# Memory at the borders between two kinds of layer, reused tile by tile

## The chip, the cores and the metric

The kernel runs on one core of one Trainium2 chip. The core has a matrix engine (TensorE: PE for the matmuls, PEld for its weight loads), a vector engine (DVE), a scalar engine (ACT), a general engine (POOL) and a sync engine (SP) whose work here is to issue DMAs. Each engine works through its own instructions in order. A DMA is issued by an engine (ACTq, SPq in the profile) and then runs by itself. The metric is the device time of one execution in microseconds (us); lower is better.

## The reference

Four layers over 2048 tokens of 640 numbers, in the order A, B, A, B; each layer is `x = x + layer(layernorm(x))`. Both kinds walk through the tokens in segments and carry a memory along.

```python
# A: 32 heads of 20, 4 segments of 512 tokens
for s in range(4):
    p = softmax(q_s k_s^T * scale + causal_mask);  a_dot = p @ v_s
    a_mem = (phi(q_s) @ M) / (phi(q_s) @ z + 1e-6)
    o_s = g * a_mem + (1 - g) * a_dot
    M += phi(k_s)^T @ v_s;  z += sum(phi(k_s))
return concat(o) @ wo
# B: 32 heads of 128, 64 segments of 32 tokens, memory of 8 rows
mem = mem0
for s in range(64):
    h = concat([mem, x_s])                      # 40 rows
    q, k, v = h @ Wq, h @ Wk, h @ Wv            # each 640 x 4096
    p = softmax(q k^T * scale masked);  o = (p @ v) @ Wo
    mem = o[:8];  out_s = o[8:]
```

A step of B needs the memory rows that the step before has made, so its 64 steps are a chain. A's last segment has no memory to hand on.

## The kernel before

**Layer A** (`layer_A`) takes a segment of 512 tokens as four tiles of 128. `seg_load` loads a tile (`a_xt`) and normalizes it (`a_xn`), `seg_tr` transposes it (`a_tps`) into `a_xnT`. Eight groups of four heads follow; a group projects Q, K, V (`a_QP`, `a_KP`, `a_VP`), spreads Q over a masked tile by four small DMAs (`a_qTm`), and works through four heads: scores `a_S`, softmax `a_Pj`, transposes `a_tpA`/`a_tpB`, `a_PVu`. The memory (`a_MZ`, `a_MZb`) is brought up to date in the first three segments only. A finished segment goes through an out stage per tile: `out_stage_a` loads the residual (`a_xr`) and transposes the result (`a_otps`, copied by ACT to `a_oT`), `out_stage_b` multiplies by Wo (`a_YP`), adds the residual (`a_xnew`) and stores it twice, as float32 (`xres`) and as bfloat16 (`xres_bf`), which is what B reads. The last segment's four out stages are A's drain. A scheduler sets the order of A's instructions on every engine.

**Layer B** (`layer_B`) has a prologue and 64 steps. The order of its instructions on PE, ACT, DVE and POOL is written out by hand, and all of them carry line 100 in the profile; the scheduler places only its DMAs on SP. B's Wq and Wk stay resident: they are loaded during the first layer. Wv and Wo (5.24 MB each) are loaded anew for each B. The prologue:

1. loads four tiles of x (`b_xt`), issues the loads of Wv and Wo on ACT's queue (`load_B_weights`), normalizes two tiles, transposes them (`b_lntps`); ACT copies them to `b_HX` (24 rows per step) and `b_TX` (the last 8 rows of each of 8 steps, the tails); five small DMAs bring in `mem0`.
2. The tails of the first 8 steps are projected with Wq and Wk in eight units (`b_tail`), evicted by ACT and DVE in turn to `b_tu` and stored to memory outside the core (`b_QKd`), from where each step takes its rows (`b_tl`).
3. K and Q of step 0 (`b_Kp`, `b_Qp`), evicted to `b_kq`, transposed (`b_TP`) and scattered to `b_KT` and `b_QT`.
4. The tails' V in eight units (`b_vtail`), evicted to `b_vt`, each stored by two DMAs (`b_VTd`); then V of step 0 (`b_V`), and the first unit of the next 8 steps.

Step 0 proper begins with the matmuls `b_Ka`, `b_Qa`, `b_Kb`, `b_Qb`. A step ends with the projection by Wo (`b_OPS`); the tail rows' own projection is deferred (`b_OPSd`), added to what was stored (`b_XOd`, a load, an add, a store).

A tile framework hands out memory. A pool holds tiles, and a tile name with `bufs` buffers makes the tile wait for the last use of the one `bufs` back. When a layer ends its pools are released, and a new pool on the same memory waits for the whole released pools below it. Both `b_tu` and `b_vt` have one buffer. At the border from B to A, A's four weights are loaded on ACT's queue (`load_A_weights`).

Of the kernel before, what the change touches and what calls it, by code (L numbers as in the profile page):

```python
# [28 lines left out]
D = 640  # L29
NCH = 5  # L30
# [105 lines left out]
def alloc_A_weights(tc, ctx, W):  # L136
    wp = ctx.enter_context(tc.tile_pool(name="a_w", bufs=1))
    W.wq = wp.tile([128, NCH, 32, 32], BF16, name="a_wq_pad")
    W.wk = wp.tile([128, NCH, 32, 32], BF16, name="a_wk_pad")
    W.wv = wp.tile([128, NCH, D], BF16, name="a_wv")  # L140
    W.wo = wp.tile([128, NCH, D], BF16, name="a_wo")


def load_A_weights(nc, W, A_wq, A_wk, A_wv, A_wo, padded, stage):

    first = not padded
    eng = nc.sync if first else nc.scalar
    for nm, src, pad in (("wq", A_wq, W.wq), ("wk", A_wk, W.wk)):
        if first:
            raw = stage[nm]  # L150
            nc.gpsimd.memset(pad[:, :, :, 20:32], 0.0)
            nc.vector.tensor_copy(pad[:, :, :, 0:20], raw.rearrange("p c (h d) -> p c h d", d=20))
        else:
            nc.scalar.dma_start(pad[:].rearrange("p c h s -> p (c h s)"), padded[nm])
    eng.dma_start(W.wv[:], A_wv.rearrange("(c p) n -> p c n", p=128))
    eng.dma_start(W.wo[:], A_wo.rearrange("(c p) n -> p c n", p=128))
# [8 lines left out]
def layer_A(nc, tc, C, W, x_src, x_dst, src_is_bf16, nseg=4, out_bf16=False, xb_dst=None, load_w=None, side_loads=None):  # L165
# [7 lines left out]
    with ExitStack() as ctx:  # L173
        st = ctx.enter_context(tc.tile_pool(name="a_state", bufs=1))
        seg = ctx.enter_context(tc.tile_pool(name="a_seg", bufs=2))
        wk = ctx.enter_context(tc.tile_pool(name="a_wk", bufs=2))
        w1 = ctx.enter_context(tc.tile_pool(name="a_wk1", bufs=1))
        up = ctx.enter_context(tc.tile_pool(name="a_unit", bufs=3))
        up2 = ctx.enter_context(tc.tile_pool(name="a_unit2", bufs=3))
        sm = ctx.enter_context(tc.tile_pool(name="a_sm", bufs=4))  # L180
        pg = ctx.enter_context(tc.tile_pool(name="a_pg", bufs=2, space=PSUM))
        pss = ctx.enter_context(tc.tile_pool(name="a_pss", bufs=3, space=PSUM))
        ppt = ctx.enter_context(tc.tile_pool(name="a_ppt", bufs=3, space=PSUM))

        MZ32 = st.tile([128, 8, 128], F32, name="a_MZ32")
        nc.vector.memset(MZ32[:], 0.0)
        MZb = st.tile([128, 8, 128], BF16, name="a_MZb")
        vaug = [st.tile([128, 4, 4, 32], BF16, name=f"a_vaug{i}") for i in range(2)]
        phik = [st.tile([128, 4, 4, 32], BF16, name=f"a_phik{i}") for i in range(2)]
# [6 lines left out]
        qTm_t = [st.tile([128, 4, 512], BF16, name=f"a_qTm{i}") for i in range(2)]  # L196
# [9 lines left out]
        def seg_load(n_, tt):  # L206
            d = SEG.setdefault(n_, {"xn": [None] * 4, "oT": [None] * 4, "xr": [None] * 4})
            r0 = n_ * 512 + tt * 128
            xt = wk.tile([128, D], BF16 if src_is_bf16 else F32, name="a_xt")
            nc.sync.dma_start(xt[:], x_src[r0:r0 + 128, :])  # L210
            xn = wk.tile([128, D], BF16, name="a_xn")
            layernorm_tile(nc, sm, C, xt[:], xn[:], "a_ln")
            d["xn"][tt] = xn

        def seg_tr(n_, tt):
            d = SEG[n_]
            if "xnT" not in d:
                d["xnT"] = seg.tile([128, NCH, 512], BF16, name="a_xnT", tag="xnT")
# [12 lines left out]
        def out_stage_a(n_, tt):  # L231
            d = SEG[n_]
            r0 = n_ * 512 + tt * 128
            xr = wk.tile([128, D], BF16 if src_is_bf16 else F32, name="a_xr")
            nc.sync.dma_start(xr[:], x_src[r0:r0 + 128, :])
            oT = wk.tile([128, NCH, 128], BF16, name="a_oT")
# [6 lines left out]
        def out_stage_b(n_, tt):  # L243
# [3 lines left out]
            if src_is_bf16:  # L247
                xnew = w1.tile([128, D], F32, name="a_xnew")
            else:
                xnew = xr  # L250
# [8 lines left out]
            xnb = w1.tile([128, D], BF16, name="a_xnb")  # L259
# [5 lines left out]
        for n in range(nseg):  # L265
            xnT = SEG[n]["xnT"]
            Onat = seg.tile([128, 4, D], BF16, name="a_Onat", tag="Onat")
# [45 lines left out]
            def proj_b(G):  # L313
# [9 lines left out]
                if n <= nseg - 2:  # L323
# [4 lines left out]
                    EK = w1.tile([128, 4, 4, 20], F32, name="a_EK")  # L328
# [66 lines left out]
            def PV_evac(u):  # L395
# [7 lines left out]
                if j == 3 and n <= nseg - 2:  # L403
                    upm = w1.tile([128, 128], F32, name="a_upm")
# [125 lines left out]
def layer_B(nc, tc, C, W, x_src, xb_src, x_dst, mem0, B_Wv, B_Wo, nsteps=64, out_bf16=False, tag=""):  # L530
# [7 lines left out]
    with ExitStack() as ctx:  # L538
        st = ctx.enter_context(tc.tile_pool(name="b_state", bufs=1))
        hp = ctx.enter_context(tc.tile_pool(name="b_hx", bufs=4))  # L540
        w2 = ctx.enter_context(tc.tile_pool(name="b_w2", bufs=2))
        wk = ctx.enter_context(tc.tile_pool(name="b_wk", bufs=1))
        sm = ctx.enter_context(tc.tile_pool(name="b_sm", bufs=2))
        kqp = ctx.enter_context(tc.tile_pool(name="b_kqp", bufs=4))
        pp = ctx.enter_context(tc.tile_pool(name="b_ps", bufs=5, space=PSUM))
        po = ctx.enter_context(tc.tile_pool(name="b_po", bufs=1, space=PSUM))
# [4 lines left out]
        selm = st.tile([128, 2, 8], BF16, name="b_sel")  # L551
        nc.vector.tensor_tensor(out=selm[:, 0, :], in0=C.identb[:, 24:32], in1=C.identb[:, 88:96], op=ALU.add)
        nc.vector.tensor_tensor(out=selm[:, 1, :], in0=C.identb[:, 56:64], in1=C.identb[:, 120:128], op=ALU.add)
        OTdef = [st.tile([128, 32, 32], BF16, name=f"b_OTdef{i}") for i in range(2)]
        XO = st.tile([64, 320], F32, name="b_XO")
        nc.vector.memset(XO[:], 0.0)
        XOd = st.tile([64, 320], F32, name="b_XOd")
        mask8 = st.tile([128, 8, 40], BF16, name="b_mask8")

        Px = st.tile([128, 16, 32], BF16, name="b_Px")  # L560
        Pm = st.tile([128, 16, 32], BF16, name="b_Pm")
        nc.gpsimd.memset(Px[:], 0.0)
        nc.gpsimd.memset(Pm[:], 0.0)
        negs = wk.tile([128, 32], F32, name="b_negs", tag="PTa")
        nc.vector.memset(negs[:], -1e9)
        maskf = wk.tile([128, 40], F32, name="b_maskf", tag="OTsb")
        nc.vector.memset(maskf[:], 0.0)

        for hh in range(2):
            m = maskf[64 * hh:64 * hh + 32, :]  # L570
            nc.gpsimd.affine_select(out=m[:, 0:32], in_=negs[64 * hh:64 * hh + 32, :],
                                    pattern=[[1, 32]], compare_op=ALU.is_gt, fill=0.0, base=0, channel_multiplier=-1)
            nc.gpsimd.affine_select(out=m[:, 8:32], in_=m[:, 8:32],
                                    pattern=[[0, 24]], compare_op=ALU.is_gt, fill=0.0, base=-7, channel_multiplier=1)
            nc.gpsimd.affine_select(out=m[:, 0:8], in_=m[:, 0:8],
                                    pattern=[[0, 8]], compare_op=ALU.is_gt, fill=-1e9, base=8, channel_multiplier=-1)
        nc.vector.tensor_copy(mask8[:], maskf[:].unsqueeze(1).to_broadcast([128, 8, 40]))
        HXz = st.tile([128, NCH, 1, 32], BF16, name="b_HXz")
        nc.gpsimd.memset(HXz[:], 0.0)
# [22 lines left out]
        def ln_norm(g):  # L602
            xt = ln_xt[g]
            layernorm_tile(nc, sm, C, xt[:], xt[:], "b_ln")
            ln_ready.append(g)

        def ln_spread(g):
# [6 lines left out]
            if half == 0:  # L614
                TX[T] = w2.tile([128, NCH, 8, 8], BF16, name="b_TX", tag="TX")
# [35 lines left out]
        def tails_load(s):  # L651
            tl = wk.tile([128, 2, 32, 8], BF16, name="b_tl", tag="tl")
# [73 lines left out]
        homes = [(wk, "xt"), (wk, "OTsb"), (w2, "KT"), (w2, "QT")]  # L726
# [3 lines left out]
        load_B_weights(nc, W, B_Wv, B_Wo)  # L730
# [27 lines left out]
        tails_copy(0, tails_load(0))  # L758
        for k in range(8):
            vtail_evac(0, k, vtail_unit(0, k), "dve" if k % 2 == 0 else "act")  # L760
# [329 lines left out]
```

## Time and profile before

| what | time |
|---|---|
| three runs | 3260.51, 3264.31, 3271.95 us (median 3264.31) |
| profiled execution | 3267.92 us, of which the span (first to last instruction) is 3266.2 us |
| PE busy, share of the span | 2860.3 us, 88% |
| DVE, ACT, POOL busy | 59%, 53%, 19% |
| DMA moved | 164.33 MB, 50 GB/s on average |

The span in 40 slices, each digit the busy share in tenths, and the clock that TensorE was granted:

```profile
PE   6888984999999999998869888849999999999987
PEclk9999996999999999999979999969999999999998
```

The slices dip at three places beside the start. These are the borders between layers: A to B near 470 to 575 us, B to A near 1625 to 1675, and A to B again near 2100 to 2210. A layer of A takes some 430 to 450 us, one of B some 1050.

### The profile page before, as it was taken

Reading aid. Unit: us, or ns where it says so; the run is one execution under the profiler, and the core shown is the slowest. Engines: PE = TensorE matmul, PEld = TensorE weight load, DVE = VectorE, ACT = ScalarE, POOL = GpSimd, SP = SyncE. Lnnn points to the kernel's source line nnn. Section 1 sums busy time; section 2 is a strip of 40 time slices with the busy share of each in tenths; the row PEclk is TensorE's granted clock in tenths of the full one; section 3 lists DMA queues with packets and bytes.
Section 4 is the critical chain, followed back from the end, with each engine's and each line's share of the span. In section 5 each row is a group of like instructions: output and inputs, shape, how many; then the busy total and the mean of one; then the engine's idle time right before and its main releaser. Section 6 shows DMA issues by size and latency. Waiting matters only on the chain.

```text
span 3266.2 us, 137871 instructions
## 1 busy us (share of the span) xinstructions
PE 2860.3 (88%) x59517; PEld 1849.8 (57%) x59612; DVE 1921.2 (59%) x5213; ACT 1720.6 (53%) x3840; POOL 615.9 (19%) x1398
## 2 busy tenths in 40 slices
PE   6888984999999999998869888849999999999987
PEld 4666653555555555555446666535555555555544
DVE  6899871555455555544468998715554555555544
ACT  4888871444444444443349888714444444444432
POOL 2133320111111111111111333201111111111111
PEclk9999996999999999999979999969999999999998
DMA  5111115111121111111030111251111111111100
GB/s 189 59 38 42 37 56 166 38 40 40 39 43 39 39 41 41 36 33 27 20 105 20 58 47 43 69 162 33 41 37 37 40 37 37 39 39 35 35 22 17
DMA packets 334865, 164.33 MB, mean 50 GB/s; under 512 B 249520, under 2 KB 322992, under 8 KB 331184
## 3 DMA queue, kind: packets, MB, share of 16 engines
q1 hardware_dynamic: 321680, 119.80, 15.5%
q10 hardware_dynamic: 12576, 35.72, 3.0%
q8 instruction: 467, 7.65, 1.0%
q14 instruction: 142, 1.16, 0.1%
HBM read 95.65 MB, written 51.38 MB: 45 GB/s over the span
## 4 chain that ended last, share of the span: by engine, by line
PE 45%; ACT 14%; DVE 11%; issue 6%; POOL 4%; DMA 4%; SPq 1%; POOLq 0%; DVEq 0%; ACTq 0%
PE b_OPS L100 9%; PE b_Ka L100 5%; PE b_Qb L100 4%; PE b_Qa L100 4%; PE b_Kb L100 4%; ACT a_Pj L351 4%; PE b_OTP L100 3%; DVE b_SP L100 3%; ACT b_KT L100 2%; ACT b_QT L100 2%; PE b_OPSd L100 2%; POOL b_Px L100 2%; ACT b_kq L100 2%; PE b_vtail L100 2%; POOL b_Pm L100 2%
## 5 line engine op out<-in xcount | busy, mean ns | idle before, releaser
L100 PEld LDWEIGHTS <-b_HX 128*32 128x32 bf16 x15360 | 390.2, 97 | 426.2 <-DVE b_HX L100 44.0
L351 ACT ACTIVATE a_Pj<-a_S,a_negm 128x128 bf16<-128x128 f32 (+3 forms) x1024 | 510.4, 549 | 58.3 <-DVE a_negm L350 52.7
L350 DVE TENSOR_REDUCE a_negm<-a_S 128x1 f32<-128x128 f32 (+3 forms) x1024 | 467.0, 482 | 75.7 <-PE a_S L348 42.1
L100 POOL TENSOR_TENSOR b_Px<-b_E,b_rs 128x256 bf16<-128x256 bf16 x128 | 78.7, 615 | 1427.4 <-DVE b_rs L100 1415.4
L346 PE MATMUL a_S<-a_kT,a_qTm 128*128 128x128 bf16 (+3 forms) x1024 | 293.5, 298 | 54.0 <-ACT a_Pj L351 40.0
L100 PE MATMUL b_OPS<-b_wo,b_OTsb 128*32 128x320 bf16 x8192 | 318.0, 309 | 13.4 <-DVE b_OTsb L100 6.4
L100 PEld LDWEIGHTS <-b_OTsb 128*32 128x32 bf16 x8192 | 215.4, 100 | 113.4 <-DVE b_OTsb L100 45.7
L100 DVE CAST b_HX<-b_MT 128x40 bf16<-128x40 f32 x124 | 24.8, 200 | 391.1 <-PE b_MT L100 391.1
L361 PE MATMUL a_tpA<-c_identb,a_Pj 128*128 128x128 bf16 x2048 | 241.1, 218 | 12.9 <-ACT a_Pj L351 3.9
L348 PE MATMUL a_S<-c_negu,c_identb 128*128 128x128 bf16 x1024 | 220.5, 218 | 0.0
L100 ACT CAST b_msb<-b_OPS 128x320 bf16<-128x320 f32 x126 | 53.6, 425 | 303.5 <-PE b_OPS L100 303.5
L100 ACT CAST b_OTsb<-b_OTP 128x320 bf16<-128x320 f32 x256 | 96.5, 429 | 185.9 <-PE b_OTP L100 185.9
L100 ACT CAST b_kq<-b_Kb 128x512 bf16<-128x512 f32 x128 | 74.9, 585 | 202.3 <-PE b_Kb L100 202.3
L100 PE MATMUL b_Ka<-b_wk,b_HX 128*32 128x512 bf16 x2520 | 162.2, 387 | 21.7 <-DVE b_HX L100 21.6
L361 PEld LDWEIGHTS <-a_Pj 128*128 128x128 bf16 x2048 | 149.1, 97 | 56.5 <-issue 14.3
L348 PEld LDWEIGHTS <-c_identb 128*128 128x128 bf16 x1024 | 98.8, 97 | 129.2 <-issue 101.1
L100 DVE TENSOR_SCALAR b_kq<-b_Qa 128x512 bf16<-128x512 f32 x128 | 88.5, 692 | 139.4 <-PE b_Qa L100 138.7
L100 ACT ACTIVATE b_E<-b_SP 128x320 bf16<-128x320 f32 x256 | 111.9, 437 | 95.9 <-DVE b_SP L100 89.0
L100 PE MATMUL b_Qa<-b_wq,b_HX 128*32 128x512 bf16 x2520 | 159.4, 382 | 0.0
L100 PE MATMUL b_Va<-b_wv,b_HX 128*32 128x512 bf16 x2520 | 159.1, 381 | 0.0
L100 DVE CAST b_OTsb<-b_OTP 128x320 bf16<-128x320 f32 x256 | 113.7, 486 | 76.4 <-PE b_OTP L100 76.4
L100 PEld LDWEIGHTS <-b_kq 128*128 128x128 bf16 x2080 | 117.7, 98 | 71.7 <-ACT b_kq L100 55.2
(195 smaller groups left out, 6307.5 us busy)
## 6 DMA issues: line engine op xcount, KB each, us to landing
b_QKd<-b_tu SPq DMA_DIRECT2D x128, 128.0 KB
b_tl<-b_QKd SPq DMA_DIRECT2D x128, 128.0 KB
b_wv<-in_B_Wv_dram ACTq DMA_DIRECT2D x2, 5120.0 KB
b_wo<-in_B_Wo_dram ACTq DMA_DIRECT2D x2, 5120.0 KB
a_qTm<-a_qT SPq DMA_DIRECT2D x256, 32.0 KB
b_VTd<-b_vt SPq DMA_DIRECT2D x256, 32.0 KB
b_Vth<-b_VTd SPq DMA_DIRECT2D x512, 16.0 KB
b_XO<-xres SPq DMA_DIRECT2D x256, 30.0 KB
```

Of the source, the lines that this page charges most:

```text
L100: r = f(*a, **k)
L346: nc.tensor.matmul(Sx[:, 0:N], lhsT=stt["qTm"][:, j, 128 * qc:128 * qc + 128], rhs=kT[:, 0:N], start=True, stop=False)
L348: nc.tensor.matmul(Sx[:, N - 128:N], lhsT=C.identb[:], rhs=C.negu[:], start=False, stop=True)
L350: nc.vector.tensor_reduce(out=negm[:], in_=Sx[:, 0:N], axis=AX.X, op=ALU.max, negate=True)
L351: nc.scalar.activation(out=Pj[:, OFFS[qc]:OFFS[qc] + N], in_=Sx[:, 0:N], func=ACT.Exp, bias=negm[:, 0:1], scale=1.0)
L361: nc.tensor.transpose(tpA[:, bi, :], Pj[:, OFFS[qc] + 128 * kc: OFFS[qc] + 128 * kc + 128], C.identb[:])
```

## The change

- All pools of both layers are made with `reuse_waits="tile"`: a new tile waits for the tiles that lay on its addresses, no longer for whole pools. The pools stand in a new order, and tiles are put into other pools, so that the addresses of one layer's early tiles are those of the other layer's early-freed tiles. The separate functions that laid out the weights are gone; `layer_A` and `layer_B` do it.
- B's Wv is loaded in five pieces of 1 MB, Wo in eight of 640 KB, A's weights as before in four; all on SP's queue and none on ACT's.
- The first four x tiles of B lie in the pool `b_x`, whose places are free in A's last segment. The masks and zeroed tiles of B's prologue are made later (`init_state`, behind the scatters of K and Q).
- The prologue's `b_tu` goes through the four buffers of `b_kq`, and `b_vt` through three places.

```diff
@@ load_A_weights
-    eng = nc.sync if first else nc.scalar
...
-            nc.scalar.dma_start(pad[:].rearrange("p c h s -> p (c h s)"), padded[nm])
-    eng.dma_start(W.wv[:], A_wv.rearrange("(c p) n -> p c n", p=128))
-    eng.dma_start(W.wo[:], A_wo.rearrange("(c p) n -> p c n", p=128))
+            nc.sync.dma_start(pad[:].rearrange("p c h s -> p (c h s)"), padded[nm])
+    nc.sync.dma_start(W.wv[:], A_wv.rearrange("(c p) n -> p c n", p=128))
+    nc.sync.dma_start(W.wo[:], A_wo.rearrange("(c p) n -> p c n", p=128))
@@ layer_A
+        def pool(name, bufs):
+            return ctx.enter_context(tc.tile_pool(name=name, bufs=bufs, reuse_waits="tile"))
+        pw = pool("a_w", 1)
...
+        pxT = pool("a_xnT", 2)
+        pxt = pool("a_xt", 2)
+        pxn = pool("a_xn", 2)
+        sml = pool("a_sml", 2)
+        ste = pool("a_ste", 1)
+        w1e = pool("a_wk1e", 1)
+        stq = pool("a_stq", 1)
+        up = pool("a_unit", 3)
...
@@ B's weights
-def load_B_weights(nc, W, B_Wv, B_Wo):
-    nc.scalar.dma_start(W.wv[:], B_Wv.rearrange("(c p) h e -> p c (h e)", p=128))
-    nc.scalar.dma_start(W.wo[:], B_Wo.rearrange("h e d -> e h d"))
+def load_B_wv(nc, W, B_Wv):
+    for c in range(NCH):
+        nc.sync.dma_start(W.wv[:, c, :], B_Wv[128 * c:128 * c + 128].rearrange("p h e -> p (h e)"))
+def load_B_wo(nc, W, B_Wo, k):
+    nc.sync.dma_start(W.wo[:, 4 * k:4 * k + 4, :], B_Wo[4 * k:4 * k + 4].rearrange("h e d -> e h d"))
@@ layer_B
+        W.wv = pool("b_wv", 1).tile([128, NCH, 4096], BF16, name="b_wv")
+        hp = pool("b_hx", 4)
+        tx = pool("b_tx", 2)
+        bx = pool("b_x", 1)
+        sml = pool("b_sml", 2)
+        kqp = pool("b_kqp", 4)
+        W.wo = pool("b_wo", 1).tile([128, 32, D], BF16, name="b_wo")
...
-        homes = [(wk, "xt"), (wk, "OTsb"), (w2, "KT"), (w2, "QT")]
+        homes = [(bx, "xt"), (bx, "XO"), (bx, "XOd"), (bx, "tl")]
...
-        load_B_weights(nc, W, B_Wv, B_Wo)
+        load_B_wv(nc, W, B_Wv)
...
-            tail_evac(0, k, "act" if k % 2 == 0 else "dve")
+            tail_evac(0, k, "act" if k % 2 == 0 else "dve", (kqp, "kq"))
...
+        for k in range(8):
+            load_B_wo(nc, W, B_Wo, k)
+        alloc_seg(0)
...
+        XO, XOd = init_state()
         tails_copy(0, tails_load(0))
...
-            vtail_evac(0, k, vtail_unit(0, k), "dve" if k % 2 == 0 else "act")
+            vtail_evac(0, k, vtail_unit(0, k), "dve" if k % 2 == 0 else "act", ("vt", "E0", "E1")[k % 3])
```

The diff moves many instructions, since the scheduler sets A's order and all DMAs. Three places matter. First ACT at the border from the first A to the first B, before (`a_oT` is the drain's copy, `b_HX` and `b_TX` the copies of B's transposed x):

```order
878 L241 COPY a_oT<-a_otps 128x640 x4
879 L100 DMA b_wv<-in_B_Wv_dram 128x5x4096
880 L100 DMA b_wo<-in_B_Wo_dram 128x32x640
881 L100 COPY b_HX<-b_lntps 128x20x24
882 L100 COPY b_TX<-b_lntps 128x5x32
883 L100 COPY b_HX<-b_lntps 128x20x24
884 L100 COPY b_TX<-b_lntps 128x5x32
885 L100 ACTIVATE b_tu<-b_tail 128x8x8x8 x2
```

The same place on ACT in the changed kernel:

```order
877 L446 COPY a_nsb<-a_NUM 128x512
878 L100 COPY b_HX<-b_lntps 128x20x24
879 L100 COPY b_TX<-b_lntps 128x5x32
880 L100 COPY b_HX<-b_lntps 128x20x24
881 L254 COPY a_oT<-a_otps 128x640 x2
882 L100 COPY b_TX<-b_lntps 128x5x32
883 L254 COPY a_oT<-a_otps 128x640
884 L100 ACTIVATE b_tu<-b_tail 128x8x8x8
885 L254 COPY a_oT<-a_otps 128x640
```

The two weight loads are gone from ACT, and B's copies and the first tail eviction stand between A's last copies.

Second, SP at the same border, before (the rows from the drain's last stores to the stores of the tails):

```order
94 L258 DMA xres<-a_xnew 128x640
95 L261 DMA xres_bf<-a_xnb 128x640
96 L258 DMA xres<-a_xnew 128x640
97 L261 DMA xres_bf<-a_xnb 128x640
98 L822 DMA b_XO<-xres 24x5x64
99 L599 DMA b_xt<-xres_bf 128x640
100 L822 DMA b_XO<-xres 24x5x64
101 L599 DMA b_xt<-xres_bf 128x640 x2
102 L737 DMA b_HX<-in_B_mem_dram 128x8x1 x5
103 L793 DMA b_XOd<-xres 32x5x64 x2
104 L599 DMA b_xt<-xres_bf 128x640
105 L689 DMA b_QKd_10080<-b_tu 128x8x64 x8
```

In the changed kernel the four `b_xt` and five `b_HX` loads stand among the `a_qTm` copies at the head of A's last segment, all of Wv and two pieces of Wo ahead of the first store of the drain's four tiles; from the third store on the rows read:

```order
103 L271 DMA xres<-a_xnew 128x640
104 L274 DMA xres_bf<-a_xnb 128x640
105 L532 DMA b_wo<-in_B_Wo_dram 128x4x640
106 L715 DMA b_QKd_10111<-b_tu 128x8x64
107 L271 DMA xres<-a_xnew 128x640
108 L274 DMA xres_bf<-a_xnb 128x640
109 L715 DMA b_QKd_10111<-b_tu 128x8x64 x3
110 L532 DMA b_wo<-in_B_Wo_dram 128x4x640
111 L715 DMA b_QKd_10111<-b_tu 128x8x64
112 L532 DMA b_wo<-in_B_Wo_dram 128x4x640 x3
113 L678 DMA b_tl<-b_QKd_10111 128x512
114 L735 DMA b_VTd_10112<-b_vt 64x256 x6
```

Stores of the tails now stand between A's last stores, and the last pieces of Wo stand ahead of the V tails' stores on the same queue.

Third, SP at the border from B to A, before:

```order
527 L782 DMA xres<-b_XO 120x1x64 x2
528 L791 DMA xres<-b_XOd 4x40x64 x2
529 L793 DMA b_XOd<-xres 32x5x64 x2
530 L791 DMA xres<-b_XOd 4x40x64 x2
531 L210 DMA a_xt<-xres 128x640 x2
532 L235 DMA a_xr<-xres 128x640 x2
533 L210 DMA a_xt<-xres 128x640 x4
```

And in the changed kernel:

```order
538 L223 DMA a_xt<-xres 128x640 x2
539 L145 DMA a_wq_pad<-a_wq_home 128x5120
540 L145 DMA a_wk_pad<-a_wk_home 128x5120
541 L811 DMA xres<-b_XO 120x1x64 x2
542 L820 DMA xres<-b_XOd 4x40x64 x2
543 L146 DMA a_wv<-in_A_wv_dram 128x5x640
544 L822 DMA b_XOd<-xres 32x5x64 x2
545 L147 DMA a_wo<-in_A_wo_dram 128x5x640
546 L223 DMA a_xt<-xres 128x640
547 L820 DMA xres<-b_XOd 4x40x64 x2
548 L223 DMA a_xt<-xres 128x640
```

Two of A's x tiles and three of its weights have moved ahead of B's last loads and stores, and the weights, which ACT issued before, stand among them.

More of the change, by code (lines that the diff above doesn't have):

```diff
@@ L186, in layer_A, with psum @@
+        wkl = pool("a_wkl", 2)
+        w1l = pool("a_wk1l", 1)
+        st = pool("a_state", 1)
+        sm = pool("a_sm", 4)
+        W.wo = st.tile([128, NCH, D], BF16, name="a_wo")
+        def psum(name, bufs):
+            return ctx.enter_context(tc.tile_pool(name=name, bufs=bufs, space=PSUM, reuse_waits="tile"))
+        pss = psum("a_pss", 3)
+        ppt = psum("a_ppt", 3)
+        pg = psum("a_pg", 2)
+        MZ32 = ste.tile([128, 8, 128], F32, name="a_MZ32")
         nc.vector.memset(MZ32[:], 0.0)
-        MZb = st.tile([128, 8, 128], BF16, name="a_MZb")
@@ L188, in layer_A @@
-        vaug = [st.tile([128, 4, 4, 32], BF16, name=f"a_vaug{i}") for i in range(2)]
-        phik = [st.tile([128, 4, 4, 32], BF16, name=f"a_phik{i}") for i in range(2)]
+        MZb = stm.tile([128, 8, 128], BF16, name="a_MZb")
+        vaug = [stm.tile([128, 4, 4, 32], BF16, name=f"a_vaug{i}") for i in range(2)]
+        phik = [ste.tile([128, 4, 4, 32], BF16, name=f"a_phik{i}") for i in range(2)]
         for i in range(2):
@@ L195, in layer_A @@
         nc.vector.memset(biasq[:], math.log(SC))
-        qTm_t = [st.tile([128, 4, 512], BF16, name=f"a_qTm{i}") for i in range(2)]
+        qTm_t = [stq.tile([128, 4, 512], BF16, name=f"a_qTm{i}") for i in range(2)]
         for i in range(2):
@@ L208, in seg_load @@
             r0 = n_ * 512 + tt * 128
[L209 to L212, printed above, removed]
+            xt = pxt.tile([128, 2 * D] if src_is_bf16 else [128, D], BF16 if src_is_bf16 else F32, name="a_xt")
+            nc.sync.dma_start(xt[:, 0:D], x_src[r0:r0 + 128, :])
+            xn = pxn.tile([128, D], BF16, name="a_xn")
+            layernorm_tile(nc, sml, C, xt[:, 0:D], xn[:], "a_ln")
             d["xn"][tt] = xn
@@ L217, in seg_tr @@
             if "xnT" not in d:
-                d["xnT"] = seg.tile([128, NCH, 512], BF16, name="a_xnT", tag="xnT")
+                d["xnT"] = pxT.tile([128, NCH, 512], BF16, name="a_xnT", tag="xnT")
             xn = d["xn"][tt]
@@ L247, in out_stage_b @@
             if src_is_bf16:
-                xnew = w1.tile([128, D], F32, name="a_xnew")
+                xnew = w1l.tile([128, D], F32, name="a_xnew")
             else:
@@ L548, in ps_tile, with psum @@
+        st = pool("b_state", 1)
+        w2 = pool("b_w2", 2)
+        wk = pool("b_wk", 1)
+        sm = pool("b_sm", 2)
+        def psum(name, bufs):
+            return ctx.enter_context(tc.tile_pool(name=name, bufs=bufs, space=PSUM, reuse_waits="tile"))
+        pp = psum("b_ps", 5)
+        po = psum("b_po", 1)
         def ps_tile(shape, dtype, name):
             return pp.tile(shape, dtype, name=name, tag="ps")
-        selm = st.tile([128, 2, 8], BF16, name="b_sel")
-        nc.vector.tensor_tensor(out=selm[:, 0, :], in0=C.identb[:, 24:32], in1=C.identb[:, 88:96], op=ALU.add)
@@ L553, in layer_B @@
[L553 to L558, printed above, removed]
         Px = st.tile([128, 16, 32], BF16, name="b_Px")
         Pm = st.tile([128, 16, 32], BF16, name="b_Pm")
-        nc.gpsimd.memset(Px[:], 0.0)
@@ L563, in layer_B @@
[L563 to L576, printed above, removed]
@@ L614, in ln_spread @@
             if half == 0:
-                TX[T] = w2.tile([128, NCH, 8, 8], BF16, name="b_TX", tag="TX")
+                TX[T] = tx.tile([128, NCH, 8, 8], BF16, name="b_TX", tag="TX")
             nc.scalar.copy(HX[g][:, :, :, 8:32], tps[:, :, :, 0:24])
```

122 lines of the change are left out of this document (61 added, 61 removed).

## The prediction

> **What bounds the kernel now.** I read the table by windows first, because the four layers have different limits and a mean over the span hides the borders. I cut the span at the last score work of a layer and at the first step of the next. Columns: window, length, PE busy, PEld, DVE, ACT, POOL, PE clock, DMA share, GB/s.
>
> ```profile
> 24.60:471.00 446.40, 390.83 (x5026) 283.01 (x5073) 389.95 (x1022) 378.75 (x863) 119.09 (x206) 0.99 0.19 59
> 471.00:574.30 103.30, 46.28 (x676) 32.68 (x674) 19.83 (x53) 11.79 (x24) 11.39 (x27) 0.68 0.49 151
> 574.30:1624.60 1050.30, 984.61 (x23909) 603.35 (x23912) 537.02 (x1492) 466.11 (x1026) 166.98 (x455) 0.99 0.18 37
> 1624.60:1672.70 48.10, 17.15 (x203) 10.29 (x200) 15.74 (x43) 5.14 (x9) 9.23 (x15) 0.58 0.46 153
> 2103.20:2207.40 104.20, 47.15 (x663) 33.56 (x663) 19.48 (x53) 11.61 (x24) 11.27 (x26) 0.66 0.50 153
> ```
>
> Inside a layer PE is busy for 88 to 94% of the time at a clock of 0.99. At the three borders, 255.6 us together, it is busy for 110.6 us, at 0.58 to 0.68. Whatever the change does, it does there; the rest of the span has the same instructions in nearly the same order.
>
> Next, the chain of waits from A's end into B's first step (start, length, what):
>
> ```profile
> 489.68 17.12 DMA b_wv<-in_B_Wv_dram
> 507.25 2.98 DMA b_HX<-in_B_mem_dram
> ...
> 514.84 13.99 DMA b_QKd<-b_tu
> ...
> 529.68 2.14 DMA b_QKd<-b_tu
> ...
> 538.41 2.27 DMA b_QKd<-b_tu
> ...
> 554.35 1.99 DMA b_VTd<-b_vt
> ...
> 566.49 3.03 DMA b_VTd<-b_vt
> ...
> 573.07 1.28 PE b_vtail L100 x10
> 574.35 2.17 PE b_Ka L100 x20
> ```
>
> Three kinds of wait fill it. First 20 us for Wv and the memory rows behind it. Then the tails of Q and K: one buffer `tu`, so each of eight evictions waits until the store of the one before has landed (13.99 us for the first, which runs beside Wo; about 2.2 us each later). Then the same for `vt` with eight V evictions. Why the tails start only at 511.8, though their inputs Wq and Wk have been resident since the first layer, the rows of ACT show (start, length, queue or engine, operation):
>
> ```profile
> 489.68 0.39 ACTq L100 DMA_DIRECT2D b_wv<-in_B_Wv_dram  x1
> 509.64 0.39 ACTq L100 DMA_DIRECT2D b_wo<-in_B_Wo_dram  x1
> 510.36 0.56 ACT L100 COPY b_HX<-b_lntps 128x480 bf16<-128x480 bf16 x1 [26.77 <-DMA b_HX<-in_B_mem_dram]
> ```
>
> ACT's instruction stream holds both weight loads ahead of the copy that makes HX. The first load can't start before A's buffers are released at 489.68, and the second is issued 19.96 us later; only then can ACT copy. So 5.24 MB cost at most 20 us, or about 260 GB/s.
>
> **A to B, both times.** The change removes the two loads from ACT, lets Wv begin when the projections of A's last group are through and Wo when its last unit's tiles are free, brings the x tiles, LN and memory rows into A's last segment, and puts 136 of 160 Wq tail matmuls ahead of A's last output projection. What stays behind that projection, I take from PE's busy time and its two groups:
>
> ```profile
> 491.00:574.30 83.30, 36.12 (x610) 26.75 (x612) 13.90 (x34) 8.53 (x19) 4.70 (x17) 0.64 0.53 161
> ```
>
> ```profile
> L100 PE MATMUL b_tail<-b_TX,b_wq 128*128 128x64 bf16 x200 | 8.5, 216 | 5.3 <-ACT b_TX L100 3.6 <-ACT b_vt L100 1.7
> ...
> L100 PE MATMUL b_tail<-b_TX,b_wk 128*128 128x64 bf16 x160 | 6.1, 209 | 0.0
> ...
> L100 PE MATMUL b_lntps<-c_identb,b_xt 128*128 128x128 bf16 x20 | 2.9, 309 | 38.9 <-DVE b_xt L100 38.9
> ```
>
> 136 tails at 8.5/200 us are 5.8 us, and 10 of 20 transposes 1.5 us: 36.1 − 5.8 − 1.5 = 28.8 us of PE work remain. The moved 7.3 us go into A's drain:
>
> ```profile
> 471.00:491.00 20.00, 10.16 (x66) 5.93 (x62) 5.93 (x19) 3.25 (x5) 6.69 (x11) 0.83 0.33 109
> ```
>
> ```profile
> 485.96 1.52 PE L254 MATMUL a_YP<-a_wo,a_oT 128*128 128x320 bf16 x10 [1.49 <-DVE a_xnew L256]
> ```
>
> It has 9.8 us idle on PE, so they fit, though not all in the gaps: I let the last projection end at 490 instead of 487.5. Then 28.8 us of PE work, and 7 us of waits that I place by hand: the last four of Wo's eight pieces are queued on SP ahead of the first VT store (4 × 0.66 MB at 260 GB/s, 10 us, of which some 6 lie under K, Q and their transposes), and the mask that now is made just before the first `vt`, about 3. Ka starts at 490 + 28.8 + 7 = 526 instead of 574.35: **gain 48 us**. The chain's waits for the stores go because four `tu` buffers and three `vt` buffers let an eviction run while three or two stores are still under way, at 2.2 us each against a new tail about every 1.5 us (6.1 us of matmuls for the four Wk units, less at a full clock).
>
> Bounds. Above: no slip, no waits, and the 28.8 us at the clock of a busy PE, by the first and the second Ka of the run:
>
> ```profile
> 574.35 2.17 PE b_Ka L100 x20
> ...
> 591.12 1.26 PE b_Ka L100 x20
> ...
> 607.25 1.26 PE b_Ka L100 x20
> ```
>
> 28.8 × 1.26/2.17 = 17, so Ka at 505, gain 69. I don't take it: PE will still stop for evictions, and its clock in this window was 0.64. Below: what if small transfers still stand behind big ones (first rival), 25.
>
> At the second A-to-B border the chain is the same with one wait exchanged:
>
> ```profile
> 2129.42 12.74 DMA b_xt<-xres_bf
> ...
> 2149.20 9.79 DMA b_QKd<-b_tu
> ...
> 2207.50 2.25 PE b_Ka L100 x18
> ```
>
> The window is 104.2 us against 103.3, PE's work in it 47.2 against 46.3. I give it the same **48 us**.
>
> **B to A.** Rows of the border:
>
> ```profile
> 1631.19 3.93 PE L100 MATMUL b_OPSd<-b_wo,b_OTdef 128*32 128x320 bf16 x64 [2.26 <-DVE b_XOd L100]
> ...
> 1634.06 1.39 SPq L793 DMA_DIRECT2D b_XOd<-xres  x2
> ...
> 1636.79 0.89 ACTq L156 DMA_DIRECT2D a_wo<-in_A_wo_dram  x1
> ...
> 1645.97 1.01 DVE L100 TENSOR_TENSOR b_XOd<-b_OPSd,b_XOd 64x320 f32<-64x320 f32 x2 [9.60 <-DMA b_XOd<-xres]
> ...
> 1650.34 0.81 SPq L210 DMA_DIRECT2D a_xt<-xres  x2
> ...
> 1656.45 0.69 PE L222 MATMUL a_tps<-c_identb,a_xn 128*128 128x128 bf16 x5 [21.34 <-DMA a_xr<-xres]
> ...
> 1666.11 0.59 PE L279 MATMUL a_QP<-a_xnT,a_wq_pad 128*128 128x512 bf16 x1 [0.78 <-ACT a_xnT L223]
> ```
>
> Two small XOd loads issued at 1634 are through only at 1646, because A's four weight loads start in the same microseconds; and A's x tiles are queued on SP behind the store that follows. In the change the first two x tiles, Wq, Wk and Wv stand ahead of the XOd loads, and the XOd add moves from 1646 to about 1639. x tiles 3 and 4 still come around it: the fourth stands behind the store after that add. Before, 1666.1 − 1650.3 = 15.8 us passed from the first x issue to QP, with two pairs of LN after one another; now one pair is done in B's last step and the other needs about 9 us. QP near 1648: **gain 18 us**. Bounds: 10, if the fourth tile's load waits for Wv and Wo as the XOd loads did; 22, if all four tiles are ready when B's last matmul ends at 1635 and only three transposes and their copies follow.
>
> **Costs.** Four x tiles (0.66 MB, 2.5 us by the rate above) and five memory loads are queued on SP ahead of the qTm copies of A's last segment:
>
> ```profile
> 366.84 0.29 POOL L444 CAST a_MZb<-a_MZ 128x128 bf16<-128x128 f32 x1
> ...
> 368.96 28.56 SPq L293 DMA_DIRECT2D a_qTm<-a_qT  x16
> ...
> 506.82 3.34 SPq L737 DMA_DIRECT2D b_HX<-in_B_mem_dram  x5
> ...
> 2123.50 5.82 SPq L737 DMA_DIRECT2D b_HX<-in_B_mem_dram  x4
> ```
>
> The x tiles lie where MZ lay, free from 366.8, so they go at once, but the SP queue is in order and the memory loads took 3.3 to 5.8 us to issue in the old place. About 2 us per A layer, since units of the segment before are still being worked off; with the LN's vector work I take −4 in all, 0 to −12. The loads of A's weights on SP in place of ACT cost SP four issues under 1 us, in B's last steps, where SP waits anyway. At the kernel's start only a few loads of the first window change places: nothing, ±1. The pools' new order itself is free in the steps.
>
> Sum: 48 + 48 + 18 − 4 = 110. The profiled execution took 3267.9 us, 3.6 above the median of 3264.3; so 3267.9 − 110 = 3157.9, and against the median 3154. I say **3155**.
>
> **The rivals.** *Small behind big* (chance 0.2): Wv and Wo now share SP's queue with QKd, VTd, the residual rows and the x tiles, and SP also stops at each piece whose place isn't free. The 13.99 us QKd wait and the 12.74 us x-tile wait show what one big transfer does to a small one, even from another queue. Against it: pieces of 0.66 and 1.05 MB last 2.5 and 4 us, and most of Wv is issued before the drain. If it holds for half the pieces at each border, the gain falls to 25 + 25 + 15 − 4 = 61: 3203. (The Trainium skill, DMA: Bandwidth & Descriptors, section Queues, rings and completion order, says that an engine switches between queue rows packet by packet while descriptors within a ring are consumed in order; by that rule one shared row is worse for the small stores than two, and this rival's time would be the one to expect. The trace agrees only in part: the two queues apart did not spare the store its 13.99 us.)
>
> *Still more* (0.15): PE stays busy over the border, its clock too. Between the forecast and the upper bound of 69: 62 + 62 + 21 − 1 = 144, 3120. For it speaks that LN, HX and TX are long ready; against it that evictions and stores remain between the groups.
>
> *The step pays* (slower, 0.04): the new homes or the tile-wise waits lengthen B's steps. 128 steps of 16.1 us (607.25 − 591.12) would have to grow by 110/128 = 0.86 us each to undo the gain; at 1.0 us the kernel would take 3264 − 110 + 128 = 3282. It decides from 0.86 us. Against it: no instruction and no wait in a steady step has moved.
>
> *Not what it says* (0.04): a tile in the address map frees last after all, Wv starts at A's end as before and, SP being in order, holds everything behind it; the borders stay as they are, within 0.3% of 3264 (about 10 us, the least that a measurement of this kernel can tell from no change).
>
> **How the numbers follow.** Forecast 0.57, the four rivals 0.43. Range 3118 to 3206: it takes in the forecast's own bounds, the first rival and the second. Faster 0.92, same 0.04, slower 0.04.
>
> **What would show it.** The wait of HX for the memory rows (26.8 us) gone; the waits of `tu` and `vt` for their stores below 10 us together; Wv landed before A's last projection; Ka about 36 us after A's last projection instead of 87; QP 13 us after B's last matmul instead of 31; Ka to Ka unchanged at 16.1. The prediction is wrong if the stores QKd and VTd still take over 5 us each, if A's drain is stretched past 495, or if qTm starts its segment late.

## The result and the profile after

| | before | changed |
|---|---|---|
| median of four runs | 3267.94 us | 3129.97 us |
| lowest to highest | 3260.51 to 3271.95 | 3125.31 to 3135.10 |
| span of the profiled execution | 3266.2 us | 3131.0 us |

The ratio is 0.9581, with a 95% interval of 0.9554 to 0.9607: the change is 4.2% faster, 138 us by the medians and 135.2 us by the two profiled spans.

The table by windows of the changed kernel, with the same columns as before (window, length, PE, PEld, DVE, ACT, POOL, PE clock, DMA share, GB/s), shows where. The first row runs from the end of A's score work to B's first Ka, the second begins with the end of A's last projection, the third is B, the fourth the border from B's last matmul to A's first QP.

```profile
470.00:513.66 43.66, 34.62 (x655) 26.52 (x652) 15.20 (x37) 11.21 (x23) 8.73 (x22) 0.90 0.76 217
...
486.70:513.70 27.00, 20.47 (x463) 16.00 (x463) 10.15 (x25) 5.93 (x13) 4.37 (x15) 1.00 0.73 205
...
513.66:1563.50 1049.84, 988.22 (x23946) 606.43 (x23948) 540.03 (x1501) 466.71 (x1028) 167.31 (x457) 0.99 0.18 38
...
1571.20:1587.80 16.60, 2.47 (x20) 1.62 (x19) 7.25 (x17) 2.77 (x4) 5.78 (x8) 0.59 0.68 213
```

The border from A to B, 103.3 us in the old table, is 43.7 us long, and PE is busy for 34.6 of them at a clock of 0.90; behind A's last projection the clock is 1.00. (At the second border from A to B, 28.6 us long, the clock is 0.94.) Cut at the same events in both traces (first QP, end of A's last projection, Ka, end of the last deferred projection, QP, and so on), the span divides like this:

| stage, us | before | changed | difference |
|---|---|---|---|
| start to first QP | 24.6 | 22.7 | −1.9 |
| A, to its last projection | 462.9 | 464.0 | +1.1 |
| border A to B | 86.8 | 27.0 | −59.8 |
| B | 1060.8 | 1057.5 | −3.3 |
| border B to A | 31.0 | 16.7 | −14.3 |
| A | 454.6 | 457.9 | +3.3 |
| border A to B | 86.7 | 28.6 | −58.1 |
| B to the end | 1058.8 | 1056.7 | −2.1 |

The columns add up to the spans, so nothing is left over. A second profile of the changed kernel gave 1051.4 us for the first B, so differences of a few us in that row are not explained by an edit. Most steps take 16.1 us from Ka to Ka in both kernels, and late steps of a B up to 17.8 in both. In the changed kernel the second and fourth step of both Bs take 17.8 too (16.1 before); in the first B of the second profile they took 16.1.

How the border looks on PE now (start, length, operation, and in brackets the idle time before it and its cause):

```profile
485.14 1.52 PE L267 MATMUL a_YP<-a_wo,a_oT 128*128 128x320 bf16 x10 [0.65 <-DVE a_xnew L269]
...
487.48 4.83 PE L100 MATMUL b_tail<-b_TX,b_wk 128*128 128x64 bf16 x160
493.78 0.45 PE L100 MATMUL b_lntps<-c_identb,b_xt 128*128 128x128 bf16 x5 [1.47 <-DVE b_xt L100]
494.17 1.26 PE L100 MATMUL b_Kp<-b_wk,b_HX 128*32 128x512 bf16 x20
...
501.14 0.40 PE L100 MATMUL b_TP<-c_identb,b_kq 128*128 128x128 bf16 x4 [1.69 <-DVE b_kq L100]
501.46 4.56 PE L100 MATMUL b_vtail<-b_wv,b_TX 128*64 128x256 bf16 x80
507.80 2.34 PE L100 MATMUL b_V<-b_wv,b_HX 128*32 128x512 bf16 x40 [1.78 <-ACT b_vt L100]
...
512.99 0.74 PE L100 MATMUL b_vtail<-b_wv,b_TX 128*64 128x256 bf16 x10 [1.58 <-DVE b_vt L100]
513.66 1.26 PE L100 MATMUL b_Ka<-b_wk,b_HX 128*32 128x512 bf16 x20
```

Four short stops, 6.5 us in all, are what is left of the old chain. The first matmuls of Ka take 1.26 us, no longer 2.17. At the second border PE's longest stop is 4.2 us:

```profile
2068.44 3.97 PE L100 MATMUL b_V<-b_wv,b_HX 128*32 128x512 bf16 x40 [4.21 <-ACT b_vt L100]
```

The waits for stores in the window from 470 to 513.7 us (engine, waiting row, cause: us in total, times, longest):

```profile
DVE b_vt L100 <- DMA b_VTd<-b_vt: 7.4, 2, 3.7
...
ACT b_vt L100 <- DMA b_VTd<-b_vt: 6.0, 2, 4.2
...
DVE b_kq L100 <- DMA b_QKd<-b_tu: 3.1, 1, 3.1
```

In this window `tu` no longer waits for any store. `vt` still waits 13.4 us on two engines, mostly beside PE's work, and one copy of Q now waits for a tail's store, since both use the `kq` buffers. At the second border (2030 to 2075 us) the same waits are longer: `vt` 18.5 us, at most 6.6 at once, `tu` 2.5, and the copies of K and Q 8.5.

SP's own rows show when the weights go out:

```profile
448.36 0.34 SPq L528 DMA_DIRECT2D b_wv<-in_B_Wv_dram  x1
...
462.15 0.42 SPq L528 DMA_DIRECT2D b_wv<-in_B_Wv_dram  x1
...
471.75 0.94 SPq L532 DMA_DIRECT2D b_wo<-in_B_Wo_dram  x2
...
495.68 3.67 SPq L532 DMA_DIRECT2D b_wo<-in_B_Wo_dram  x3
...
504.41 3.70 SPq L735 DMA_DIRECT2D b_VTd<-b_vt  x6
```

Wv's last piece is issued at 462, 23 us before A's last projection, where the old kernel issued its first byte at 489.7.

At the border from B to A, the rows of the last deferred sum and of the x tiles:

```profile
1571.55 1.43 SPq L822 DMA_DIRECT2D b_XOd<-xres  x2
1573.09 0.75 SPq L147 DMA_DIRECT2D a_wo<-in_A_wo_dram  x1
1573.89 1.05 SPq L223 DMA_DIRECT2D a_xt<-xres  x1
1576.65 1.01 DVE L100 TENSOR_TENSOR b_XOd<-b_OPSd,b_XOd 64x320 f32<-64x320 f32 x2 [7.96 <-DMA b_XOd<-xres]
1577.68 1.30 SPq L820 DMA_DIRECT2D xres<-b_XOd  x2
...
1579.03 0.49 SPq L223 DMA_DIRECT2D a_xt<-xres  x1
...
1587.85 0.59 PE L292 MATMUL a_QP<-a_xnT,a_wq_pad 128*128 128x512 bf16 x1 [0.78 <-ACT a_xnT L236]
```

The sum is ready 5 us after its load is issued, where it was 12; but the fourth x tile is issued only behind the store that follows the sum.

### The profile page after: what moved, and what is told of

Read it like the earlier page. It is cut to its first block, busy times and chain, and to the rows that moved or that the text cites. A ratio compares the mean times of both kernels' runs of the same rounds, so it can differ in the third digit from the quotient of the medians.

```text
span 3131.0 us, 137798 instructions
## 1 busy us (share of the span) xinstructions
PE 2833.5 (90%) x59517; PEld 1835.8 (59%) x59612; DVE 1921.1 (61%) x5213; ACT 1723.6 (55%) x3840; POOL 616.7 (20%) x1398
## 3 DMA queue, kind: packets, MB, share of 16 engines
q1 hardware_dynamic: 333168, 145.03, 18.5%
## 5 line engine op out<-in xcount | busy, mean ns | idle before, releaser
L100 ACT CAST b_kq<-b_Ka 128x512 bf16<-128x512 f32 x128 | 75.0, 586 | 150.7 <-PE b_Ka L100 150.7
```

Source lines behind the costliest of these rows:

```text
L100: r = f(*a, **k)
```

## The experiments

The runs below compare with the kernel before on the same chip. The changed kernel itself, run again beside some of them, gave 0.9583 (0.9567 to 0.9598).

> The changed kernel itself, for a ratio beside the next three on one chip. Every theory: 0.958 of the time before, about 3131.

### One buffer each for `tu` and `vt`

```diff
-            tail_evac(0, k, "act" if k % 2 == 0 else "dve", (kqp, "kq"))
+            tail_evac(0, k, "act" if k % 2 == 0 else "dve")
...
-            vtail_evac(0, k, vtail_unit(0, k), "dve" if k % 2 == 0 else "act", ("vt", "E0", "E1")[k % 3])
+            vtail_evac(0, k, vtail_unit(0, k), "dve" if k % 2 == 0 else "act")
```

> The change with one thing undone: the prologue's tu and vt have one buffer each again. Theory (waits first, the clock follows): at both A-to-B borders the stores come back one after the other. The eight tu evictions can start in the drain (about 479 us) but take 8 x 2.9 us and more beside Wo's pieces, the eight vt evictions about 3 us each, so Ka comes near 538 instead of 513.7: 25 us lost per border, about 3180 us, and the granted clock in the last 25 us before Ka falls below 0.8. Rival (the early loads alone bring the gain, the buffers hide nothing): within 10 us of 3130, clock about 1.00.

Measured: 3206.2 us, ratio 0.9806 (0.9792 to 0.9821). Some 75 us are lost against the change, not 50. Its borders from A to B are 64.3 and 61.4 us long. The window of the first, and PE's rows in it:

```profile
486.00:550.30 64.30, 28.73 (x465) 19.63 (x461) 12.64 (x31) 7.12 (x15) 4.94 (x16) 0.68 0.32 86
```

```profile
502.50 0.72 PE L100 MATMUL b_lntps<-c_identb,b_xt 128*128 128x128 bf16 x5 [15.77 <-DVE b_xt L100]
...
517.87 0.72 PE L100 MATMUL b_lntps<-c_identb,b_xt 128*128 128x128 bf16 x5 [8.63 <-DVE b_xt L100]
...
549.08 1.28 PE L100 MATMUL b_vtail<-b_wv,b_TX 128*64 128x256 bf16 x10 [3.13 <-DVE b_vt L100]
```

DVE normalizes the third and the fourth x tile between two evictions, so a `tu` that is late also holds LN, and through it PE for 15.8 and 8.6 us. I had not counted that. The clock is 0.68 in this window and 0.73 in its last 25 us, as the theory had it, and the rival (no loss) is out.

The edit does more than its name says. It also moves `tu` from the pool `b_kqp` back to `b_wk`. ACT's first eviction, in this run and then in the change:

```profile
495.24 0.60 ACT L100 ACTIVATE b_tu<-b_tail 128x512 bf16<-128x512 f32 x1 [14.72 <-DMA xres_bf<-a_xnb]
```

```profile
479.89 0.60 ACT L100 ACTIVATE b_tu<-b_tail 128x512 bf16<-128x512 f32 x1 [2.88 <-PE b_tail L100]
```

Here it waits 14.7 us for the store of A's last `a_xnb`, by the profile, so it looks as if the new place of `tu` is one that A leaves last; at the second border the same wait is 14.0 us. The first eviction comes 15.3 us later than in the change, and the stop of 15.8 us hangs on it. So the 37.3 us that the first border loses are the price of the buffers' number and of this place together, and no run separates the two.

### The rotating evictions alone

The kernel before with the two lines above and the helpers' `home` argument, nothing else.

> The kernel before with only the rotating evictions (tu through the four kq buffers, vt through three places); weights still on ACT's queue at the border, x tiles late, old pools. Theory: the waits for HX (26.8 us) and the start at 511.8 stay, the store waits go; 33 us of PE work at the half clock and some 5 us of waits follow, Ka near 549 instead of 574: 25 us gained per border, about 3215 us. Rival (store waits are only in front of a wait for Wv and Wo, which would end last anyway): less than 10 us gained per border, above 3245.

Measured: 3224.8 us, ratio 0.9859 (0.9842 to 0.9875). 44.5 us are gained, against some 50 expected; its first border is 64.8 us long. Two waits hold it, from the waits of that window:

```profile
ACT b_HX L100 <- DMA b_HX<-in_B_mem_dram: 26.6, 1, 26.6
...
DVE b_tu L100 <- DMA b_QKd<-b_tu: 10.2, 1, 10.2
ACT b_tu L100 <- DMA b_QKd<-b_tu: 10.0, 2, 8.6
```

HX waits as before, and four buffers are not enough while all of Wo runs: an eviction then waits up to 10.2 us for a store.

Put together, at the first border from A to B: rotation alone takes 22.0 us off it, the rest of the change with single buffers 22.5, both 59.8. **Each leaves the wait that the other removes.** Whether the 15.3 us beyond the sum come from taking away both is open: the first eviction of the single `tu` comes 15.3 us late because of its place, and that alone could make them up.

### The default waits of a reused pool

```diff
-            return ctx.enter_context(tc.tile_pool(name=name, bufs=bufs, reuse_waits="tile"))
+            return ctx.enter_context(tc.tile_pool(name=name, bufs=bufs))
```

(and the same in the other three places).

> The change with the default waits of a reused pool (a new tile waits for the whole released pools below it) in place of the tile-wise ones; order on every engine and all addresses are unchanged. Theory: the new pools are small and lie in the order in which they fall free, so a pool's last use is close to its tile's last use; at most 5 us lost per border, 3130 to 3145. Rival (the tile-wise waits carry the gain): the first B tiles wait for A's last users again, the loads slip to A's end, 20 us or more lost per A-to-B border, above 3170.

Measured: 3136.4 us, ratio 0.9593 (0.9578 to 0.9607), which overlaps with the change; its borders in the trace are 27.0, 14.7 and 29.3 us long against 27.0, 16.7 and 28.6. So with this order of pools, the tile-wise wait gives nothing that these runs can tell. What is left to let the loads start early is the order of many small pools, together with the new queue; no run undoes that order alone.

### B's weights on ACT's queue

```diff
-        nc.sync.dma_start(W.wv[:, c, :], ...)
+        nc.scalar.dma_start(W.wv[:, c, :], ...)
...
-    nc.sync.dma_start(W.wo[:, 4 * k:4 * k + 4, :], ...)
+    nc.scalar.dma_start(W.wo[:, 4 * k:4 * k + 4, :], ...)
```

> The change with B's 13 weight pieces issued by ACT and not by SP (the scheduler puts Wv's five between A's last softmax work, Wo's eight behind the K casts of the prologue). Theory (what counts is that the loads start early and that ACT isn't held): the small stores aren't hurt by sharing SP's queue, so nothing is won there, and ACT loses some 4 us of issue and Wo runs beside the V tails' stores: 3130 to 3145. Rival (on one queue the small transfers stand behind the big ones): the waits that are left before Ka, about 6 us per border, go, and it is faster than the change by 5 to 12 us: 3118 to 3125.

Measured: 3163.7 us, ratio 0.9675 (0.9661 to 0.9690): over 30 us slower than the change, worse than either side expected. A's first layer is 9 us longer (473.2 against 464.0), with Wv's issues among the softmax work on ACT. The five issues themselves take 1.7 us there, so what held the layer is open. The borders are 35.2 and 41.8 us. ACT's rows, and the row of PE that waits for them:

```profile
507.37 12.87 ACTq L100 DMA_DIRECT2D b_wo<-in_B_Wo_dram  x8
520.29 0.86 ACT L100 COPY b_QT<-b_TP 128x384 bf16<-128x384 bf16 x2 [12.49 <-DMA b_VTd<-b_vt]
520.82 3.41 PE L100 MATMUL b_vtail<-b_wv,b_TX 128*64 128x256 bf16 x30 [7.24 <-ACT b_QT L100]
521.03 0.67 ACT L100 CAST b_vt<-b_vtail 128x256 bf16<-128x256 f32 x2
```

and DVE's wait for a store of `vt`:

```profile
527.49 0.42 DVE L100 CAST b_vt<-b_vtail 128x256 bf16<-128x256 f32 x1 [14.92 <-DMA b_VTd<-b_vt]
```

Eight issues of Wo one behind the other hold ACT for 12.9 us, and the Q copies wait behind them (the profile puts that idle time down to a store, since issuing is not counted as work); PE stops for 7.2 us. The issues themselves take 4.2 of the 12.9; the rest are two pauses of 3.0 and 5.5 us between them, for which the trace names no cause. DVE's 14.9 us are mostly the same stop: the buffer it waits for is filled by ACT's eviction at 521.03, which stood behind the issues (the fifth unit takes the place of the second), and from the issue of that buffer's stores at 521.45 it takes 6.0 us. With everything on SP's queue the longest wait of `vt` for a store is 4.2 us at the first border and 6.6 at the second. So these runs do not show that a separate queue protects the small stores or harms them; they show that the issues cost ACT its own work. The rival, which expected a gain, is out.

### Half of Wo behind the V tails' stores

```diff
-        for k in range(8):
+        for k in range(4):
             load_B_wo(nc, W, B_Wo, k)
...
+        for k in range(4, 8):
+            load_B_wo(nc, W, B_Wo, k)
         for b in range(2):
             ps = thin_mm(cols, W.wv, b, "b_V")
```

> The change with the last four pieces of Wo (2.6 MB, 8 to 10 us) issued behind the sixteen stores of the V tails and not ahead of them. Theory A (the waits left before Ka are the engines' own turn-taking, the V-tail stores are hardly held by Wo): the first waits before V shrink by at most 2 us a border and the projection by Wo, 13 us after Ka, begins to wait for its last pieces: 3130 to 3145. Rival (the small stores stand behind the big pieces in SP's queue): the waits of vt for its stores (13.4 us before) fall below 5, Ka comes 4 us or more earlier at each border: 3120 to 3125.

Measured: 3132.6 us, ratio 0.9590 (0.9574 to 0.9606), as the change; the borders are 27.1 and 29.7 us. The wait of `vt` for its stores is 13.8 us in all (13.4 before the edit). These four pieces ahead of the V tails' stores cost nothing here that can be measured; the pieces that stand among the stores of the tails were not moved.

### A's weights behind the fourth x tile

```diff
-            if tt == 1:
+            if tt == 3:
                 load_w()
```

> The change with A's weight loads behind the fourth x tile's load in the program; on SP the x tiles 3 and 4 then stand right beside the XOd loads and Wv and Wo behind them. Theory (the 16.7 us from B's last matmul to QP are the XOd load, then two x tiles after one another behind it): tile 4 no longer waits for the store after the XOd add, QP comes 4 to 7 us earlier: 3124 to 3127, with Wv needed only after QP and KP. Rival (QP waits for B's last sums because the transposes need the banks that the XOd add frees, whatever the loads do): less than 2 us earlier.

Measured: 3127.3 us, ratio 0.9569 (0.9556 to 0.9583). The rows that show it:

```profile
1572.51 0.50 SPq L223 DMA_DIRECT2D a_xt<-xres  x1
1573.43 1.38 SPq L822 DMA_DIRECT2D b_XOd<-xres  x2
1574.87 0.48 SPq L223 DMA_DIRECT2D a_xt<-xres  x1
...
1583.63 0.59 PE L292 MATMUL a_QP<-a_xnT,a_wq_pad 128*128 128x512 bf16 x1 [0.78 <-ACT a_xnT L236]
```

Both x tiles go out by 1575 and QP follows 8.5 us after B's last matmul, 8 us sooner than in the change. Part of that is where the border is taken to begin: the last deferred projection ran from 1570.65 for 4.46 us here, in the change from 1568.79 for 2.36. Counted from the end of the last step's own projection (`b_OPS`), QP follows after 17.7 us in place of 22.6, and 22.0 to 24.2 in the other runs that leave this border as the change has it: some 5 us sooner, within the 4 to 7 expected. The whole run is 3.4 us faster than the change beside it, and the intervals overlap, so the border's gain is shown and its effect on the whole time only made likely.

### The masks ahead of K and Q

The call of `init_state` moved from behind the scatters to the line ahead of `cols = cols_of(0)`.

> The change with the masks and zeroed tiles (init_state) made ahead of K and Q of step 0, as before the change, instead of behind their scatters. My step counted about 3 us per border for the mask ahead of the first vt. If that was right, Ka comes 2 to 3 us earlier at each of two borders: 3125 to 3128. Rival (DVE and POOL have time there, the vt waits are for VT's stores): within 2 us of the change; or later, if the memory of these tiles is freed late and DVE stands in front of it.

Measured: 3129.7 us, ratio 0.9579 (0.9566 to 0.9592): no change. The borders are 26.2 and 27.5 us against 27.0 and 28.6; the mask costs about 1 us there, not 3.

### Both of the last two

> The change with A's weight loads behind the fourth x tile and the masks made ahead of K and Q. In the traces the first edit took 8 us from the B-to-A border, the second about 1 us from each A-to-B border and nothing else: 10 us, 3120 to 3123, ratio 0.955. Rival (what is saved at a border is lost in the layer behind it): as the change, 0.958.

Measured: 3124.6 us, ratio 0.9571 (0.9557 to 0.9585). The borders in its trace are 26.0, 8.4 and 29.2 us. By the ratios it is 0.12% below the change, some 4 us, no better than the weights' order alone (0.9569), and the intervals overlap: the lowest median of all, and not proved better. The 10 us expected counted the 8 us of the border in full, of which some 5 are an earlier QP.

### Extra matmuls that keep PE awake

The kernel with one `tu` and one `vt`, and in its prologue matmuls whose results nobody reads:

```diff
+        fps = po.tile([128, 320], F32, name="b_fill", tag="opsd")
+        def fill(n):
+            for _ in range(n):
+                nc.tensor.matmul(fps[:], lhsT=C.identb[:], rhs=W.wq[:, 0, 0:320], start=True, stop=True)
         for k in range(8):
             tail_unit(0, k, 0, 8, shared=True)
+            if k >= 3:
+                fill({3: 72, 7: 40}.get(k, 12))
...
             vtail_evac(0, k, vtail_unit(0, k), "dve" if k % 2 == 0 else "act")
+            fill(12)
```

> The run with one tu and one vt buffer, and in its prologue extra matmuls into an unused bank (72 of 128x320 after the fourth tail unit, 12 or 40 after the others, 12 after each V unit), whose results nobody reads: they keep PE busy while it waits for stores, so that its clock stays up, and change no wait. Theory (waits first; the clock only prices what lies between them): the clock in the 64 us before Ka rises from 0.68 to above 0.9, K and Q of step 0 go from 7.4 to about 5 us, Ka comes 3 to 6 us earlier: 3206 falls to 3195 to 3200. Rival (the low clock was what made the border long, and the stores fill the gaps it leaves): 15 us or more per border, below 3178.

Measured: 3199.3 us, ratio 0.9796 (0.9781 to 0.9810), against 0.9806 without the extra matmuls. Its border's window, and one group of it:

```profile
486.00:549.00 63.00, 57.30 (x700) 39.96 (x698) 12.47 (x31) 7.12 (x15) 5.66 (x17) 0.95 0.34 92
```

```profile
L100 PE MATMUL b_Kp<-b_wk,b_HX 128*32 128x512 bf16 x40 | 2.5, 380 | 0.0
```

The clock is 0.95 in place of 0.68, and the 40 matmuls of Kp take 2.5 us in place of 3.8. The border is 62.8 us long, 1.5 less than without. But the run doesn't price the clock alone: from 503 us to Ka its chain of work that ended last lies on PE, and the extra matmuls themselves are 37.7% of that chain from 486 to 552 us. In the kernel without them PE has 13 us of the chain from 486 us to Ka; at the lengths that the same matmuls have here it would have some 8. So by an estimate from the two traces, a full clock is worth about 5 of the 64 us. The rival's 15 us or more is not borne out by that estimate, though the measured time alone doesn't rule it out. The stores keep their pace either way: PE makes a V unit every 2.4 us here, and still the seven evictions of `vt` before Ka span 19.2 us, against 19.7 without.

## Why the prediction was right, and what it mis-sized

Forecast were 3155 us and a range of 3118 to 3206; 3130 is in it, and the sign and the place were right. The gain came to 135 us by the spans, where 110 was forecast. By the terms of the sum:

- **A to B, forecast 48 each, measured 59.8 and 58.1.** This is the step that was mis-sized. Ka was put at 526 and came at 513.7. Of the 12.3 us, 8.3 lie in "28.8 us of PE work remain": the remaining matmuls took 20.5 us. I had priced them by PE's busy time in the old window, that is at a clock of 0.64, and moved the instructions into a place where the clock is 1.00. Another 3.3 us lie in "the last projection ends at 490": it ended at 486.7, since the 136 tails fitted into the drain's gaps. The third part, 7 us of waits, measured 6.5, and that is luck: I had placed them in Wo's last pieces ahead of the V stores and in the mask, and the experiments found nothing that could be measured for the first and about 1 us for the second. The four stops of PE wait for LN of the fourth x tile, a copy of Q and two evictions of `vt`. The second border hides the same luck: its PE work is 21.8 us and its stops are 6.8.
- **The bound of 69 and why I didn't take it.** I wrote that "PE will still stop for evictions". It does: at the first border four times, for at most 1.8 us, and the clock was 1.00; at the second for up to 4.2 us, and the clock was 0.94. So the stops came as I wrote, and the step from them to a clock of 0.64 was wrong: once the long waits go, the matmuls between them must be priced at the clock that they will then have.
- **Which wait went.** Both that I named, and each would have kept most of the border: 64.8 us with the old loads, 64.3 with single buffers (up to 15.3 of which the place of `tu` may have cost). My sum took them away together, rightly; the experiment with a single `tu` showed two things that I had not named: LN of the third and fourth x tile hangs on the evictions, and the evictions hang on when A frees the memory under `tu`.
- **The signs to look for.** Wv was out long before the last projection, and no wait of HX for the memory rows is left. Ka came 27 us after A's last projection, where I expected 36, and QP 16.7 us after B's last matmul, where I expected 13. I expected the waits of `tu` and `vt` below 10 us together; they are 13.4 at the first border and 21.0 at the second, mostly beside PE's work. Of the signs of being wrong, A's drain did not stretch (486.7) and qTm did not start late (363.8); stores over 5 us can't be excluded, since a wait for one reaches 6.6 at the second border. The mask, for which I counted 3 us, is worth about 1.
- **B to A, forecast 18, measured 14.3.** The mechanism was right, and two sizes were not. The XOd sum came 5.5 us after B's last matmul, where 1639 meant 4; and "the other pair needs about 9 us" was 11, as the fourth x tile stands behind the store of that sum. With the loads in another order QP comes some 5 us sooner, so here too the order on SP's queue sets it.
- **Costs, forecast −4, measured −4.4** in the two A layers, but not as 2 and 2. The first A's 1.1 us are within its spread (463.1 to 465.4 in the runs that keep the change's A, 463.7 in the old layout with rotation), the second A's 3.3 are not (457.5 to 460.8 against 454.6 and 455.3). No run took the loads ahead of qTm away again, so that they are the cause is not shown. The start gave 1.9 us that I had put at nothing. The 5.4 us from the two B layers are within what two profiles of one kernel differ by.
- **The rivals.** *Still more* came nearest: its 3120 is 10 us off, the forecast 25. I gave it 0.15, because I held that the stops between the groups would keep PE and its clock down. *Small behind big* fell as a matter of the time: with half of Wo moved behind the V stores nothing changed, and with the weights on another queue the kernel was slower. The rule of order within one ring, cited there from the Trainium skill (DMA: Bandwidth & Descriptors, Queues, rings and completion order), did not decide the time. At the first border the core's DMA traffic falls from some 360 GB/s to below 90 near 505 us, where the stores of `vt` begin (504.4), so the pieces were through. *The step pays* fell with most steps at 16.1 us and both Bs no longer than before. *Not what it says* fell with Wv's first issue at 448.

That the tile-wise waits, the first words of the change, carry the gain was never tested by my sum; the run with the default waits shows that they do not, with these pools.

## What to carry to other kernels

When two waits follow each other and each is long, take both away before judging either: here each alone gave 22 us of a border of 87, and both together gave 60. When you undo one part of a change, look at what else the edit moves: here the single buffer also changed its place in memory, and that may be the 15 us between the two sums. Price matmuls that leave a stalled window at the clock of the place they go to, and not by the stalled window's busy time. Move big loads to where their memory falls free, in pieces, and onto an engine that has no compute work behind them.

## What the runs showed of the hardware that was not expected

- Eight loads of 640 KB issued one after the other held ACT's instruction stream for 12.87 us. The issues took 0.38 to 1.01 us each, 4.2 in all; in the two pauses between them, 3.0 and 5.5 us, ACT did nothing else. On SP two of them took 0.94 us and three 3.67.
- With the load's pieces on the stores' own queue, started earlier, evictions of `vt` waited at most 4.2 us for a store at the first border and 6.6 at the second; with the pieces on another queue one buffer's stores took 6.0 us from their issue to the next eviction.
- With PE kept busy by idle matmuls its granted clock rose from 0.68 to 0.95 over the same 63 us, and the border was 1.5 us shorter, with those matmuls themselves on the chain that ended last.
